# An output product with eleven matmuls for twelve, and a filter product with its constants as weights

## The chip, the cores and the metric

The kernel runs on one core of one Trainium2 chip. The metric is the device time of one execution in microseconds. Several executions are timed, and the median counts. One more execution is recorded by the profiler. The engines have short names in the profile: PE (the matrix engine, PEld its weight loads), DVE (vector), ACT (scalar, here the exponentials), POOL, and SP, which mainly starts transfers.

## The reference

Two independent branches have their results put side by side. Sizes: S = 2048 positions, D = 448 features, H = 16 heads of Dh = 28.

```
# A: attention with 16 query heads and one shared key and value head
q = (A_x @ A_wq) in 16 heads;  k = A_x @ A_wk;  v = A_x @ A_wv
p = softmax(q @ k.T * Dh**-0.5)          # per head, 2048 x 2048
a = concat over heads(p @ v) @ A_wo
# B: a filter in the frequency domain, over positions and features
b = irfft2(rfft2(B_x) * (B_w_r + 1j*B_w_i))
return concat([a, b], axis=-1)           # 1 x 2048 x 896, float32
```

## The kernel before

**Opening.** In the first 70 us an explicit planner (class `Plan`) orders the projections of queries, keys and values, and the first transforms of the filter. Products that must be exact to float32 are made of float32r parts: a number x becomes a high part (x cast to float32r) and a low part (x minus that), and three products stand for one: high by high, low by high, high by low. A float32r product is one matmul record in the profile. A plain float32 product is two records.

**Attention loop.** The 2048 queries are four chunks c of 512, the 16 heads four groups g of four heads. Each of the 16 pairs (c, g) has 16 steps, one for each 128 keys: 256 steps. A step has four scores (`score`, L1100: 128 keys by 512 queries, float32r), four exponentials on ACT (L1117, from a PSUM bank to a buffer p in SBUF, of which there are `P_BUFS`), and four value products (`values`, L1132, float32, each in its own 32 columns of the array, so that the four run side by side). The values of a group add up in bank 7. DVE copies it out (`group_out`), POOL carries the row sums through DRAM and back as a tile R, with transfers that spread each sum over 32 rows, and `group_norm` multiplies by 1/sum and splits the result into `oh` and `ol`. A head occupies 32 rows of these tiles: 28 of results, one with the sum, three spare.

**Filler.** Two more kinds of PE work are cut into pieces and put between scores by `fill`. An output unit (`w_unit`, 12 of them: three chunks of four blocks of 128 positions; L1020) has four pieces, one for each group, of three float32r matmuls of 448 columns (`oh` by `woh`, `ol` by `woh`, `oh` by `wol`, where `woh` and `wol` are the parts of the output weights). The last chunk's output products for groups 0 to 2 run at the very end. The last transforms of the filter have units in two stages, 16 of each: `z_unit` (L942) goes over positions, four float32 products of 128 columns; `y_unit` (L961) over features, four float32 products of 113 columns with the data as weights and the constants `cs3` streaming. DVE then combines the four results (L966 to L975), and SP stores them to `ob`. Before that, DVE has done a transform over the 32 residues and the filter's weights on a tile X, as background work up to about 310 us.

**Order.** The loop at the end of the kernel fixes the order of every engine when the program is built. It keeps clocks of its own for PE, DVE and ACT (`clk`), a time for each bank to come free (`free`), and a heap of later work (`after`). It writes the values of `n` steps at once, a *round*, where `size` makes n four if more than 1 us of filler is ready, else two. After each round `share` sets how much filler the next may take: at least 1.6 us, or the rest spread over the remaining steps. `LEAD` is how many scores run ahead of a round. Each engine then executes its list in order.

Of the kernel before, what the change touches and what calls it, by code (L numbers as in the profile page):

```python
# [12 lines left out]
F32 = mybir.dt.float32  # L13
F32R = mybir.dt.float32r
# [3 lines left out]
ALU = mybir.AluOpType  # L18
# [5 lines left out]
DH = D // H  # L24
# [7 lines left out]
P_BUFS = 20  # L32
# [63 lines left out]
def kernel(ctx: ExitStack, tc: tile.TileContext, t: dict):  # L96
# [14 lines left out]
    X = cp.tile([128, 2, 32, 113], F32, name="X")  # L111
# [101 lines left out]
    with tc.tile_pool(name="f1", bufs=2) as f1[0], tc.tile_pool(name="w1", bufs=1) as w1, ExitStack() as ctx1:  # L213
# [146 lines left out]
        def load_const(name, shape):  # L360
            def go():
                cons[name] = cp.tile(shape, F32, name=name)
                nc.sync.dma_start(cons[name], t[name])
            return add(SP, 0.4, go, loads[1, 1], kb=32)
# [297 lines left out]
    pp = ctx.enter_context(tc.tile_pool(name="pp", bufs=P_BUFS))  # L662
    V = nc.vector
# [27 lines left out]
    woh = ap.tile([128, NG, D], F32R, name="woh", bufs=1)  # L691
    wol = ap.tile([128, NG, D], F32R, name="wol", bufs=1)
    fc["cs3"] = ap.tile([113, 4, 113], F32, name="cs3", bufs=1)
    nc.gpsimd.dma_start(fc["cs3"], t["cs3"])
# [214 lines left out]
    Xf = X.rearrange("p r n f -> p (r n f)")  # L909
    taken = [0]  # L910

    def carve(p, n):
        o = taken[0]
        taken[0] += n
        return Xf[:p, o:o + n]

    c2t = [carve(128, 904).rearrange("p (u j f) -> p u j f", u=2, f=113) for _ in range(2)]
    fit = [carve(128, 512).rearrange("p (j f) -> p j f", f=128) for _ in range(2)]
    zt = [[carve(113, 512).rearrange("p (r j n) -> p r j n", r=2, n=64) for _ in range(2)] for _ in range(2)]
    mt = [carve(128, 226).rearrange("p (k f) -> p k f", f=113) for _ in range(2)]  # L920
    y1t = [carve(128, 452).rearrange("p (k h f) -> p k h f", k=2, f=113) for _ in range(2)]
    yot = [carve(128, 452).rearrange("p (k f) -> p k f", f=113) for _ in range(2)]
# [6 lines left out]
    def fft3_load(q):  # L929
        if q > 7:  # L930
            return
        nc.gpsimd.dma_start(c2t[q % 2].rearrange("p u j f -> p u (j f)"), t2[:, :, 452 * q:452 * q + 452])
        nc.gpsimd.dma_start(fit[q % 2], t["fi"][:, 4 * q:4 * q + 4])
        after(clk["dve"] + (10.0 if q < 2 else 6.0), 0.0, work["z"].extend, [z_unit(q, 0), z_unit(q, 1)])

    def z_unit(q, e):
        w = (113, 112)[e]

        def go(b):
            pz = view(bank[b], 4, 128)  # L940
            for j in range(4):
                mm(pz[:w, j], c2t[q % 2][:, e, j, :w], fit[q % 2][:, j], start=True, stop=True)  # L942
            if e == 1:
                after(clk["pe"] + 1.2, 0.0, fft3_load, q + 2)
            after(clk["pe"] + 1.2, 0.72, out, b)

        def out(b):
            V.tensor_copy(zt[q % 2][e][:w], view(bank[b], 4, 128)[:w].rearrange("p j (r n) -> p r j n", r=2))  # L948
# [3 lines left out]
        return [(0.88, go)]  # L952

    def y_unit(q, v):
        js = slice(2 * v, 2 * v + 2)

        def go(b):
            py = view(bank[b], 4, 113)
            ze, zo = zt[q % 2]
            for k, (z, w, r) in enumerate(((ze, 113, 0), (zo, 112, 0), (zo, 112, 1), (ze, 113, 1))):  # L960
                mm(py[:, k], z[:w, r, js], fc["cs3"][:w, k], start=True, stop=True)  # L961
            after(clk["pe"] + 1.2, 1.2, out, b)

        def out(b):
            py, m, y1 = view(bank[b], 4, 113), mt[v], y1t[v]
            V.tensor_copy(m, py[:, 2:4])  # L966
            TT(y1[:, :, 0], py[:, 0:2], m, op=ALU.add)
            TT(y1[:, :, 1], py[:, 0:2], m, op=ALU.subtract)
            free[b] = clk["dve"] + 0.1
            after(clk["dve"], 0.8, last)  # L970

        def last():
            y1, yo = y1t[v], yot[v]
            TT(yo[:, 0:2], y1[:, 0], y1[:, 1], op=ALU.add)
            TT(yo[:, 2:4], y1[:, 0], y1[:, 1], op=ALU.subtract)  # L975
            r0 = (2 * q + v) * 128
            nc.sync.dma_start(t["ob"][r0:r0 + 128], yo)
        return [(0.88, go)]


    oh, ol, osb = {}, {}, {}
# [13 lines left out]
    def group_sums(c, g, rs, rd):  # L995
        V.reciprocal(rs, rs)
        nc.gpsimd.dma_start(rd.rearrange("i (a b) -> (i a) b", b=16), rs)
        R = ap.tile([128, CW], F32, name="R", bufs=1)
        for i in range(4):
            nc.gpsimd.dma_start(R[32 * i:32 * i + 32], rd[i:i + 1].to_broadcast([32, CW]))  # L1000
        after(clk["dve"] + 12.0, 2.1, group_norm, c, g, R)

    def group_norm(c, g, R):
# [4 lines left out]
        TT(o, o, R, op=ALU.mult)  # L1008
        h = oh[c][:, g]
        V.tensor_copy(h, o)  # L1010
        TT(ol[c][:, g], o, h.bitcast(F32), op=ALU.subtract)
        normed[c] += 1
        if normed[c] == NG and c < NC - 1:
            after(clk["dve"] + 0.3, 0.0, work["w"].extend, [w_unit(c, k) for k in range(4)])

    def wo_mm(p, c, k, gs):
        s = slice(k * 128, k * 128 + 128)
        for g in gs:
            for n, (x, w) in enumerate(((oh, woh), (ol, woh), (oh, wol))):
                mm(p, x[c][:, g, s], w[:, g], start=(g == 0 and n == 0), stop=(g == NG - 1 and n == 2))  # L1020
# [20 lines left out]
    def w_unit(c, k):  # L1041
        def go(g):
            def f(b):
                wo_mm(bank[b][:, :D], c, k, (g,))
                if g == NG - 1:
                    after(clk["pe"] + 0.9, 0.65, out, b)
            return f

        def out(b):
            wo_out(bank[b][:, :D], c, k)  # L1050
            free[b] = clk["dve"] + 0.1
        return [(0.605, go(g)) for g in range(NG)]
# [102 lines left out]
    for g in range(NG):  # L1155
        after(w0 + 6 * g, 0.0, wo_load, g)
        after(w0 + 6.0 + 6 * g, 1.1, wo_split, g)
# [81 lines left out]
    nc.sync.dma_start(w3, t["wo"][:, g])  # L1239
# [69 lines left out]
def _layout(A_x, A_wq, A_wk, A_wv, A_wo, B_x, B_w_r, B_w_i):  # L1309
# [13 lines left out]
    z["wo"] = wo.reshape(NG, 128, D).transpose(1, 0, 2)  # L1323
# [18 lines left out]
def _gather(oa, ob):  # L1342
    out = np.empty((1, S, 2 * D), np.float32)
    out[0, :, :D] = oa
    y = ob.reshape(32, 64, 4, 113).transpose(1, 0, 2, 3).reshape(S, 4, 113)
# [9 lines left out]
_OUTS = {"oa": (S, D), "ob": (S, 4, 113)}  # L1355
# [16 lines left out]
```

## Time and profile before

| | |
|---|---|
| Median of three runs (lowest, highest) | 641.86 us (641.53, 643.83) |
| Profiled execution: time, span | 641.98 us, 640.1 us |
| Granted PE clock | 0.999 |
| Busy: PE, PEld | 633.5 us (99%), 358.5 us (56%) |
| Busy: ACT, DVE, POOL | 547.0 us (85%), 333.3 us (52%), 89.1 us (14%) |
| Transfers | 62.41 MB, mean 98 GB/s |

The span is the time from the first to the last instruction of the profiled execution, and the 1.9 us beside it lie around it. A line number names a line of the kernel before. In groups of the profile a tile is given by the name with which it was made, so the small tiles carved out of X are called X there.

### The profile page before, as it was taken

The page shows a single profiled execution, that of the slowest core. Times are in us where ns is not written, and L with a number is a line of the kernel's source. Part 1 is how long each engine was busy: PE and PEld are TensorE (multiplying, and loading weights), DVE is VectorE, ACT ScalarE, POOL GpSimd, SP SyncE. Part 2 cuts the span into 40 slices and gives each one's busy share as a digit, 9 for nine tenths or more (in the row PEclk, how much of TensorE's full clock was granted, in tenths as well). Part 3 has the DMA queues.
Part 4 walks back from the last instruction along what each step waited for, and adds up shares of the span by engine and source line. Part 5 has one row for each costly group of instructions (what it writes and reads, how often), then busy time and mean ns, then how long its engine had stood idle before and what let it go on. Part 6 is the DMA issues. An engine that isn't in the chain of part 4 may idle for free.

```text
span 640.1 us, 11636 instructions
## 1 busy us (share of the span) xinstructions
PE 633.5 (99%) x4380; PEld 358.5 (56%) x4380; DVE 333.3 (52%) x687; ACT 547.0 (85%) x1100; POOL 89.1 (14%) x164
## 2 busy tenths in 40 slices
PE   9999999999999999999999999999999999999997
PEld 7877544444444456554446655655665655564445
DVE  5999615979897977896323222215334310320014
ACT  4644899999999998889999879878888987888991
POOL 1021131101121101010122020020301101020200
PEclk9999999999999999999999999999999999999999
DMA  8766587030334121124444231132415131130002
GB/s 299 255 164 166 134 239 244 18 68 17 97 105 102 42 68 47 32 67 150 151 141 139 64 91 36 49 111 88 115 61 143 32 82 32 50 93 1 19 0 87
DMA packets 29667, 62.41 MB, mean 98 GB/s; under 512 B 6798, under 2 KB 18415, under 8 KB 28645
## 3 DMA queue, kind: packets, MB, share of 16 engines
q1 hardware_dynamic: 21850, 40.36, 23.1%
q0 software_dynamic: 7328, 20.72, 10.8%
q8 instruction: 35, 0.57, 0.4%
q10 hardware_dynamic: 432, 0.57, 0.3%
q14 instruction: 22, 0.18, 0.1%
HBM read 29.63 MB, written 15.02 MB: 70 GB/s over the span
## 4 chain that ended last, share of the span: by engine, by line
PE 88%; ACT 0%; issue 0%; DVE 0%; ACTq 0%
PE b L1100 41%; PE b L1132 36%; PE b L1020 6%; PE b L961 2%; PE b L942 2%; PE b L1252 0%; PE b L163 0%; ACT yb L1035 0%; DVE yb L1038 0%; ACTq L1036 0%
## 5 line engine op out<-in xcount | busy, mean ns | idle before, releaser
L1117 ACT ACTIVATE p<-b 128x512 f32<-128x512 f32 x1024 | 506.7, 768 | 46.4 <-PE b L1100 45.4
L1100 PE MATMUL b<-qa,ka 128*128 128x512 f32 x1024 | 284.7, 411 | 0.5 <-PEq L617 0.5
L1100 PEld LDWEIGHTS b<-qa,ka 128*128 128x128 f32 x1024 | 182.1, 188 | 128.2 <-ACT p L1117 83.9
L1132 PE MATMUL b<-p,vs 128*32 128x512 f32 x2048 | 240.0, 597 | 0.0
L1132 PEld LDWEIGHTS b<-p,vs 128*32 128x32 f32 x2048 | 56.5, 109 | 120.9 <-issue 119.3
L986 DVE COPY qraw<-b 128x512 f32<-128x512 f32 x15 | 10.4, 692 | 82.0 <-PE b L1132 82.0
L1024 DVE COPY ya<-b 128x448 f32<-128x448 f32 x12 | 7.5, 624 | 65.1 <-PE b L1020 64.0
L991 POOL DMA_DIRECT2D sd<-qraw x15 | 8.8, 587 | 218.8 <-DVE qraw L986 218.8
L827 DVE SCALAR_TENSOR_TENSOR X<-w,X 128x226 f32<-128x226 f32 (+2 forms) x72 | 34.1, 473 | 2.4
L1000 POOL DMA_DIRECT2D R<-rd x60 | 30.2, 508 | 34.9 <-DMA rd<-rs 34.9
L966 DVE COPY X<-b 128x226 f32<-128x226 f32 x16 | 6.2, 390 | 45.3 <-ACT p L1117 43.9
L321 ACT ACTIVATE qraw<-b 128x512 f32<-128x512 f32 x16 | 9.4, 599 | 19.5 <-PE b L317 19.4
L948 DVE COPY X<-b 113x512 f32<-113x512 f32 (+1 forms) x16 | 11.1, 691 | 28.6 <-ACT p L1117 22.7
L317 PE MATMUL b<-xh,wqh 128*128 128x512 f32 x64 | 24.6, 416 | 0.4 <-DVE xh L265 0.4
L1008 DVE TENSOR_TENSOR qraw<-qraw,R 128x512 f32<-128x512 f32 x15 | 10.3, 685 | 26.7 <-DMA R<-rd 26.7
L317 PE MATMUL b<-xh,wql 128*128 128x512 f32 x64 | 23.0, 390 | 0.0
L1020 PE MATMUL b<-woh,oh 128*128 128x448 f32 x60 | 22.1, 369 | 0.0
L1020 PE MATMUL b<-wol,oh 128*128 128x448 f32 x60 | 22.0, 366 | 0.0
L1020 PE MATMUL b<-woh,ol 128*128 128x448 f32 x60 | 21.9, 366 | 0.0
L820 DVE SCALAR_TENSOR_TENSOR w<-X 128x113 f32<-128x113 f32 (+2 forms) x56 | 17.7, 353 | 0.1
L961 PEld LDWEIGHTS b<-cs,X 113*128 113x128 f32 (+1 forms) x128 | 16.8, 191 | 1.4
L317 PE MATMUL b<-xl,wqh 128*128 128x512 f32 x48 | 17.3, 391 | 0.0
(113 smaller groups left out, 511.4 us busy)
## 6 DMA issues: line engine op xcount, KB each, us to landing
qa<-qa SPq DMA_DIRECT2D x15, 512.0 KB
X<-t POOLq DMA_DIRECT2D x16, 452.0 KB, 5.4
xb<-xb SPq DMA_DIRECT2D x8, 512.0 KB
qa<-qh SPq DMA_DIRECT2D x60, 64.0 KB
qa<-ql SPq DMA_DIRECT2D x60, 64.0 KB
R<-rd POOLq DMA_DIRECT2D x60, 64.0 KB, 2.2
t<-bs SPq DMA_DIRECT2D x16, 226.0 KB
wf<-w POOLq DMA_DIRECT2D x8, 452.0 KB, 4.2
```

What stands on the lines that cost most here:

```text
L317: mm(pq[c, g], w[:, j, gs], x[:, j], start=(j == 0 and n == 0), stop=(j == 3 and n == 1))
L820: STT(out, y, sy, x, op0=ALU.mult, op1=ALU.add if c > 0 else ALU.subtract)
L827: todo(226 * n, lambda d=d, q=q: STT(both(d), t[0].rearrange("p r n f -> p r (n f)"), q, both(a), op0=ALU.mult, op1=ALU.add))
L942: mm(pz[:w, j], c2t[q % 2][:, e, j, :w], fit[q % 2][:, j], start=True, stop=True)
L948: V.tensor_copy(zt[q % 2][e][:w], view(bank[b], 4, 128)[:w].rearrange("p j (r n) -> p r j n", r=2))
L961: mm(py[:, k], z[:w, r, js], fc["cs3"][:w, k], start=True, stop=True)
L986: V.tensor_copy(o, bank[7])
L1000: nc.gpsimd.dma_start(R[32 * i:32 * i + 32], rd[i:i + 1].to_broadcast([32, CW]))
L1020: mm(p, x[c][:, g, s], w[:, g], start=(g == 0 and n == 0), stop=(g == NG - 1 and n == 2))
L1100: mm(bank[b], ka[:, kc * 128:(kc + 1) * 128], qa[c, g][:, h], start=True, stop=True)
L1117: nc.scalar.activation(p, bank[b], AF.Exp, scale=SCALE)
L1132: mm(bank[7][32 * i:32 * i + 32], vs[:, kc], pt.pop(4 * st + i), start=(kc == 0), stop=(kc == 15))
```

## The change

**Eleven for twelve.** For the first three chunks the product of `ol`, group 0, by `woh` is no longer a matmul of its own. Its 16 heads' worth of rows (four heads of 28 rows, 112) are moved into the spare rows of seven other tiles: four rows of each head's 32 in `oh` for four groups and in `ol` for groups 1 to 3. To that end `ol` of group 0 is stored to DRAM (`lows`) by SP, and when group 3 is done eight small copies bring it back, after which the units become ready 7.0 us later by the planner's clock instead of 0.3. R now has 28 rows a head, with zeros in the rest from one memset. The weights get three further tiles (`woh` has 7 entries) whose spare rows hold the weights of group 0; they are loaded and split between 84 and 102 us on the planner's clock.

**Constants as weights.** `y_unit` now has the constants, split into `csh` and `csl`, as weights, and the data of `z_unit`, split into `zh` and `zl` by DVE, streaming: two sums of three float32r products, 256 columns each. The results are combined in two steps into whole blocks of 113 by 512 (`yo`) and stored as such; the host's gathering is fitted to it.

**Room.** X no longer has a place for the whole program: it lies in a pool of its own, which is closed when the last transforms begin, and their tiles take that place. `P_BUFS` goes from 20 to 17. The planner's numbers are fitted (a unit's pieces 0.403 and 0.605, 0.73 for the second filter product, at least 1.8 us of filler a round).

```diff
-P_BUFS = 20
+P_BUFS = 17
...
     def wo_split(g):
         V.tensor_copy(woh[:, g], wo[g])
-        TT(wol[:, g], wo[g], woh[:, g].bitcast(F32), op=ALU.subtract)
+        if g < NG:
+            TT(wol[:, g], wo[g], woh[:, g].bitcast(F32), op=ALU.subtract)
...
+    def fft3_open():
+        xp.close()
+        p3 = xp.enter_context(tc.tile_pool(name="p3", bufs=2))
...
+        cs = scratch()[:113, :452].rearrange("p (k f) -> p k f", k=4)
+        nc.gpsimd.dma_start(cs, t["cs3"])
+        todo(452, lambda: V.tensor_copy(csh, cs))
+        todo(452, lambda: TT(csl, cs, csh.bitcast(F32), op=ALU.subtract))
...
         def out(b):
-            V.tensor_copy(zt[q % 2][e][:w], view(bank[b], 4, 128)[:w].rearrange("p j (r n) -> p r j n", r=2))
+            pz = view(bank[b], 4, 128)[:w].rearrange("p j (r n) -> p r j n", r=2)
+            h, l = (x[:w] for x in fb["z", q % 2, e])
+            V.tensor_copy(h, pz)
+            TT(l, pz, h.bitcast(F32), op=ALU.subtract)
...
         def go(b):
-            py = view(bank[b], 4, 113)
-            ze, zo = zt[q % 2]
-            for k, (z, w, r) in enumerate(((ze, 113, 0), (zo, 112, 0), (zo, 112, 1), (ze, 113, 1))):
-                mm(py[:, k], z[:w, r, js], fc["cs3"][:w, k], start=True, stop=True)
-            after(clk["pe"] + 1.2, 1.2, out, b)
+            py = view(bank[b], 2, 256)
+            for k in range(2):
+                kind, e, r = ((0, 0, 0), (2, 1, 1), (1, 1, 0), (3, 0, 1))[2 * v + k]
+                w = (113, 112)[e]
+                zh, zl = (x[:w, r].rearrange("p j n -> p (j n)") for x in fb["z", q % 2, e])
+                for n, (c, z) in enumerate(((csh, zh), (csh, zl), (csl, zh))):
+                    mm(py[:113, k], c[:w, kind], z, start=(n == 0), stop=(n == 2))
+            after(clk["pe"] + 1.2, 2.65 if v else 1.25, out, b)
...
-        if normed[c] == NG and c < NC - 1:
-            after(clk["dve"] + 0.3, 0.0, work["w"].extend, [w_unit(c, k) for k in range(4)])
+        if c < NC - 1:
+            if g == 0:
+                lows[c] = dp.tile([128, CW], F32, name="lows", bufs=2)
+                nc.sync.dma_start(lows[c], ol[c][:, 0].bitcast(F32))
+            rows = lows[c].rearrange("(i m r) n -> r i m n", i=4, r=4)
+            if g == NG - 1:
+                for r in range(4):
+                    nc.sync.dma_start(oh[c][DH + r::32].bitcast(F32), rows[r, :, :4])
+                    nc.sync.dma_start(ol[c][DH + r::32, 1:].bitcast(F32), rows[r, :, 4:7])
+                after(clk["dve"] + 7.0, 0.0, work["w"].extend, [w_unit(c, k) for k in range(4)])
 
     def wo_mm(p, c, k, gs):
         s = slice(k * 128, k * 128 + 128)
         for g in gs:
-            for n, (x, w) in enumerate(((oh, woh), (ol, woh), (oh, wol))):
-                mm(p, x[c][:, g, s], w[:, g], start=(g == 0 and n == 0), stop=(g == NG - 1 and n == 2))
+            spare = c < NC - 1
+            for n, (x, w, m) in enumerate(((oh, woh, g), (oh, wol, g), (ol, woh, g + 3 * spare))):
+                if n < 2 or g or not spare:
+                    mm(p, x[c][:, g, s], w[:, m], start=(g == 0 and n == 0), stop=(g == NG - 1 and n == 2))
...
-    total = 12 * 4 * 0.605 + 32 * 0.88
+    total = 12 * 2.22 + 16 * (0.88 + 0.73)
 
     def share(n):
-        return max(1.6, n * (total - done[0]) / max(250 - done_steps, 3)) if n > 2 else 0.0
+        return max(1.8, n * (total - done[0]) / max(250 - done_steps, 3)) if n > 2 else 0.0
```

**The order.** Up to the 80th step PE and ACT have the same lists in both kernels. From there they part. On PE, the first output unit of the kernel before, between scores (L1100) of the round behind step 80:

```order
L1020 MATMUL b_80<-woh,oh 128x448
L1020 MATMUL b_80<-woh,ol 128x448
L1020 MATMUL b_80<-wol,oh 128x448
L1100 MATMUL b_81<-qa_1163,ka 128x512
L1100 MATMUL b_82<-qa_1163,ka 128x512
L1020 MATMUL b_80<-woh,oh 128x448
L1020 MATMUL b_80<-woh,ol 128x448
L1020 MATMUL b_80<-wol,oh 128x448
```

The same unit in the changed kernel (L1044; L1124 are the scores), which stands two rounds of two steps later, behind step 84:

```order
L1044 MATMUL b_78<-woh,oh 128x448
L1044 MATMUL b_78<-wol,oh 128x448
L1124 MATMUL b_80<-qa_1167,ka 128x512
L1124 MATMUL b_81<-qa_1167,ka 128x512
L1044 MATMUL b_78<-woh,oh 128x448
L1044 MATMUL b_78<-wol,oh 128x448
L1044 MATMUL b_78<-woh,ol 128x448
```

The first piece has two products, each later one three. Next on PE, the round of four steps that ends at step 204 in the kernel before, with two units of the second filter product in it (cs and X are the constants and the data carved from X; x4 are four products). The value products close the round: x16 for four steps, x8 for two.

```order
L1100 MATMUL b_79<-qa_128,ka 128x512
L961 MATMUL b_81<-cs_1092,X 128x113 x4
L1100 MATMUL b_82<-qa_128,ka 128x512
L1100 MATMUL b_77<-qa_128,ka 128x512
L961 MATMUL b_83<-cs_1092,X 128x113 x4
...
L1100 MATMUL b_78<-qa_128,ka 128x512
L1132 MATMUL b_84<-p,vs 32x512 x16
```

The place ahead of step 204 in the changed kernel, a round of two steps without filler:

```order
L1156 MATMUL b_83<-p,vs 32x512 x8
L1124 MATMUL b_79<-qa_127,ka 128x512
L1124 MATMUL b_82<-qa_127,ka 128x512
...
L1124 MATMUL b_79<-qa_127,ka 128x512
L1156 MATMUL b_83<-p,vs 32x512 x8
```

And its first unit of the second filter product, behind step 134:

```order
L972 MATMUL b_77<-zh_3809,csh 113x256
L972 MATMUL b_77<-zl_3810,csh 113x256
L972 MATMUL b_77<-zh_3809,csl 113x256
L972 MATMUL b_77<-zh_3811,csh 113x256
L972 MATMUL b_77<-zl_3812,csh 113x256
L972 MATMUL b_77<-zh_3811,csl 113x256
```

Four products of 113 columns have become six of 256. Counted over PE's list the loop has 30 rounds of four steps and 68 of two before, 23 and 82 now. Before, the steps from 128 to 204 are nineteen rounds of four; now those from 188 to 212 are twelve rounds of two with no filler between. At the end, six output products stand in the last round before and 33 behind the last values, now three and 36. On SP, ahead of the query copies for the next group (L206), the changed list has the copies into the spare rows:

```order
L207 DMA qa_1167<-qa_1167 64x2048
L1034 DMA oh<-lows 4x4x512
L1035 DMA ol<-lows 4x3x512
L1034 DMA oh<-lows 4x4x512
L1035 DMA ol<-lows 4x3x512
...
L206 DMA qa_127<-qh 32x512
L206 DMA qa_127<-ql 32x512
```

Four pairs of them stand there for each of the first three chunks.

More of the change, by code (lines that the diff above doesn't have):

```diff
@@ new lines, in go @@
+            after(clk["pe"] + 1.2, 2.65 if v else 1.25, out, b)
+        def out(b):
+            py = view(bank[b], 2, 256)[:113]
+            y = y1[v] = scratch()[:113, :768].rearrange("p (s n) -> p s n", s=3)
+            V.tensor_copy(y[:, 2], py[:, 1])
+            TT(y[:, 0], py[:, 0], y[:, 2], op=ALU.add)
+            TT(y[:, 1], py[:, 0], y[:, 2], op=ALU.subtract)
+            free[b] = clk["dve"] + (-1.3 if v else 0.1)
+            if v:
+                a, c = y1.pop(0), y1.pop(1)
+                for h, op in enumerate((ALU.add, ALU.subtract)):
+                    last(h, op, a, c)
@@ L982, with last @@
+        def last(h, op, a, c):
+            yo = fp.tile([113, 2, 256], F32, name="yo", tag="bs")
+            TT(yo, a[:, :2], c[:, :2], op=op)
+            nc.sync.dma_start(t["ob"][q, h], yo)
+        return [(0.73, go)]
+    oh, ol, osb, lows = {}, {}, {}, {}
+    R = ap.tile([128, CW], F32, name="R", bufs=1)
+    after(12.0, 0.4, V.memset, R, 0.0)
     normed, taken_out = [0] * NC, [0]
@@ L1051, in out @@
             free[b] = clk["dve"] + 0.1
-        return [(0.605, go(g)) for g in range(NG)]
+        return [(0.605 if g else 0.403, go(g)) for g in range(NG)]
     def switch(mode):
@@ L1154 @@
     w0 = 5.0 if FIRST == 8 else 28.0
-    for g in range(NG):
-        after(w0 + 6 * g, 0.0, wo_load, g)
-        after(w0 + 6.0 + 6 * g, 1.1, wo_split, g)
+    for g in range(7):
+        at = w0 + 6 * g if g < NG else 60.0 + 6 * g
+        after(at, 0.0, wo_load, g)
+        after(at + 6.0, 1.1, wo_split, g)
     for q in range(FIRST, 8):
```

72 lines of the change are left out of this document (28 added, 44 removed).

## The prediction

> **What bounds the kernel now.** I read the page first: its busy times and the chain that ended last.
>
> ```profile
> span 640.1 us, 11636 instructions
> PE 633.5 (99%) x4380; PEld 358.5 (56%) x4380; DVE 333.3 (52%) x687; ACT 547.0 (85%) x1100; POOL 89.1 (14%) x164
> PE 88%; ACT 0%; issue 0%; DVE 0%; ACTq 0%
> ```
>
> The matrix engine is occupied for 99% of the span, and the chain runs through it almost without a break. A busy PE may still be a waiting one, so I went on to the chain in order of time, where each piece ends when the next begins. One round of the attention loop from 397.43, and ahead of it a filter piece of the round before, with the scores behind it:
>
> ```profile
> 392.99 0.88 PE b L961 x8
> 393.87 0.48 PE b L1100 x2
> ...
> 397.43 3.57 PE b L1132 x32
> 401.00 1.59 PE b L1100 x6
> 402.59 0.60 PE b L1020 x3
> 403.19 0.45 PE b L1100 x2
> 403.65 0.62 PE b L1020 x3
> 404.27 0.46 PE b L1100 x2
> 404.73 0.87 PE b L942 x8
> 405.60 1.42 PE b L1100 x6
> 407.02 3.57 PE b L1132 x32
> ```
>
> L1132 are the value products of four steps (a full-fp32 product shows as two records, so x32 is 16 products), L1100 the scores, L1020 the output product, L942 and L961 the filter's first and second product of its last transform. Everything stands back to back: the round lasts 407.02 - 397.43 = 9.59 us, and its pieces add up to that. So each microsecond of filler taken from PE is worth up to a microsecond here. Without its filler this round is 3.57 + 1.59 + 0.45 + 0.46 + 1.42 = 7.49 us. A score costs 0.46 / 2 = 0.23, an output product about 0.61 / 3 = 0.205, and a second filter product (four fp32 products) 0.88, plus 0.02 that the two scores behind it take longer (0.48 against 0.46): 0.90.
>
> Not all rounds are of four steps. The planner makes rounds of two steps where no filler is ready; here is one before the first output products and one after them:
>
> ```profile
> 227.27 2.04 PE b L1100 x8
> 229.31 1.85 PE b L1132 x16
> ...
> 278.86 2.11 PE b L1100 x8
> 280.96 1.85 PE b L1132 x16
> ```
>
> Two such rounds do the attention work of one four-step round, and take 2 x (2.11 + 1.85) = 7.92 us late, 2 x (2.04 + 1.85) = 7.78 early, against 7.49. The turns between scores and values are paid twice. This is the row on which the argument hangs, since the change alters the number of rounds.
>
> Where does PE wait? In the rounds that hold the first output products the last run of scores is stretched:
>
> ```profile
> 235.51 1.63 PE b L1100 x5
> ...
> 245.05 1.69 PE b L1100 x6
> ...
> 254.66 1.68 PE b L1100 x6
> ...
> 264.27 1.91 PE b L1100 x7
> ...
> 274.11 1.18 PE b L1100 x5
> ```
>
> Five scores take 1.18 at 274.11 and 1.63 at 235.51; six take 1.42 at 405.60 and 1.69 and 1.68 here; seven should take 1.65 and take 1.91. That is 0.45 + 0.27 + 0.26 + 0.26 = 1.24 us in which a score waits for a bank that an exponential has not read yet. ACT is the second limit, and close.
>
> **The change part by part.** *Output product.* The order of PE has eleven products in each of the twelve units (three chunks of four) instead of twelve; all have 448 columns as before. Twelve products of 0.205 go: -2.46 us.
>
> *Second filter product.* A unit was four fp32 products (0.90 us); it becomes six fp32r products of 256 columns. No row has an fp32r product of 256 columns. The nearest are the 0.205 of 448 and the 0.23 of 512 columns. In proportion they give 0.117 and 0.115, a straight line through both 0.13; I take 0.12, which makes 0.72 a unit. As bounds serve 0.87 / 8 = 0.109, which each of the eight fp32 records at 404.73 took with a weight load of its own, and 0.205, if nothing is saved by the fewer columns. The 16 units save 16 x (0.90 - 0.72) = 2.88 us; with the bounds 16 x 0.25 = 4.0 saved, or 16 x 0.33 = 5.3 lost. The Trainium skill, page "TensorE: Matmul & The Clock Gate", Part 1, has back-to-back products at N / 2.4 GHz plus about 2.5 ns, and measures 215.7 ns at 512 columns. The rows above give 230 for those, so the trace does not agree, being 14 ns a product slower. By that rule a 256-column product would take 109 ns, an estimate from the page, and the sum below would come out 1.1 us lower.
>
> *Rounds.* In the order of PE the loop has 30 four-step and 68 two-step rounds before, 23 and 82 now: there is less filler, it is spread at 1.8 us a round at least instead of 1.6, and the outputs of a chunk become ready later, so it runs out sooner. Seven four-step rounds turn into fourteen. One of these pairs stands ahead of the first output (0.29), six behind it (7.92 - 7.49 = 0.43): 0.29 + 6 x 0.43 = +2.87 us. This eats more than half of what the products give. With the early price for all seven it is 2.0.
>
> *Waits.* The four rounds with the first outputs now carry 11 output products instead of 9, that is 0.41 us more PE work each, where a round waited 0.26 to 0.45. I let the 1.24 us go: -1.24, with 0 as the one bound. The other bound is -2.2, since the long rounds later (17 scores with two L942 pieces) may hold a further microsecond of small gaps that I cannot lay on single rows.
>
> *Fewer probability buffers, 17 for 20.* ACT in the rounds around 397:
>
> ```profile
> 391.87 6.47 ACT L1117 ACTIVATE p<-b 128x512 f32<-128x512 f32 x13 [1.16 <-PE b L1100]
> 398.50 1.57 ACT L1117 ACTIVATE p<-b 128x512 f32<-128x512 f32 x3 [0.16 <-PE b L1132]
> 401.47 6.47 ACT L1117 ACTIVATE p<-b 128x512 f32<-128x512 f32 x13 [1.39 <-PE b L1100]
> ```
>
> At 398.50 ACT waited for the values (L1132) to give a buffer back, then did three, and from about 400.1 it idled 1.39 us for new scores. With three buffers fewer it stops three exponentials earlier, and these come after the release instead: 3 x 0.48 = 1.44 us of work into a hole of 1.39. Cost nothing, as long as that hole covers it; a two-step round asks for 8 + 7 = 15 buffers at most, under 17. This cover is thin, and is a rival below.
>
> *Spare rows through DRAM.* Per chunk one store and eight small copies on SP's queue, 27 in all, and the units wait for them. The rows for their price are the last operand of group (1,0) on DVE, the first output product, and on SP's queue the last of eight copies with the copy that waits for it:
>
> ```profile
> 222.56 0.69 DVE L1011 TENSOR_TENSOR ol<-qraw,oh 128x512 fp32r<-128x512 f32 x1
> ...
> 232.74 0.61 PE b L1020 x3
> ...
> 332.62 0.59 SPq L207 DMA_DIRECT2D qa<-ql  x1
> 335.60 0.50 SPq L208 DMA_DIRECT2D qa<-qa  x1
> ```
>
> Eight issues of 0.59 are 4.7 us, and landing takes 335.60 - 333.21 = 2.4: the rows are there at about 223.25 + 7.1 = 230.4. The order puts the first output two two-step rounds later than before, near 232.7 + 7.8 = 240.5. Ten microseconds of cover: cost nothing. Queued behind the eight copies are the query copies of the next group, which come 4.7 us later; the kernel builds them a whole group ahead.
>
> *DVE.* Its nearest rows, with a stretch of the filter's last transform:
>
> ```profile
> L948 DVE COPY X<-b 113x512 f32<-113x512 f32 (+1 forms) x16 | 11.1, 691 | 28.6 <-ACT p L1117 22.7 <-PE b L942 5.9
> 400.00:450.00 50.00, 50.00 (x333) 30.25 (x326) 14.60 (x29) 41.05 (x84) 6.70 (x12) 1.00 0.29 83
> 322.85 0.69 DVE L1008 TENSOR_TENSOR qraw<-qraw,R 128x512 f32<-128x512 f32 x1 [12.86 <-DMA R<-rd]
> ```
>
> The first product's result is now cast and subtracted, so up to 0.69 more for each of 16 units, 11 us on an engine (the third figure with a count in the stretch's row) that was busy for 14.60 us of those 50. The constants' load and split fall where DVE stood 12.86 us for another transfer. Cost nothing; without such cover 0.69 a unit, 11 us. POOL's new loads stand among transfers that PE does not wait for.
>
> *End.* The last round loses three output products and the tail behind the last values gains three, 0.62 each way: nothing, or +0.6 if the last exponentials hold the round anyway.
>
> The sum: -2.46 - 2.88 + 2.87 - 1.24 = -3.71 us. The profiled execution took 641.98 us, its span 640.1 and 1.9 around it, and is 0.12 above the median of the three runs, 641.86. So 638.3 us, 0.56% under the median. A measurement of this kernel can tell about 0.5% (3.2 us) from no change, so the forecast lies just beyond what can be told.
>
> **The rivals.** *First, the second filter product saves nothing.* If the weight loads are not hidden behind so short a stream and a product takes 0.15, six take 0.90, and the sum is -0.83: 641.2 us, no change. For it speaks that a load lasts longer than the stream of 256 columns:
>
> ```profile
> L942 PEld LDWEIGHTS b<-X x128: 173/177/178, 336.6 to 534.3; 128*113 128x113 f32 x64, 128*112 128x112 f32 x64
> ```
>
> Against it, eight of just these loads with their products passed in 0.87 us, so 0.177 of span overlaps to 0.109. The Trainium skill, page "TensorE: Matmul & The Clock Gate", section "Weight-path perf modes", turns its fast weight load on only for weights of 128 columns that are not FP32. By that rule the new weights, 113 wide, load slowly, like the L942 ones, whose loads the trace shows overlapped.
>
> *Second, slower: the load is laid bare.* At 0.205 a product a unit takes 1.23, the 16 lose 5.28 where I have 2.88 gained, and the sum is +4.45: 646.4. It decides from 0.159 a product (sum zero); 3.2 us slower needs 0.192. The same overlap speaks against it.
>
> *Third, slower: too few buffers.* If the release comes later than the hole allows, every four-step round is longer by it. At 0.30 us late the 23 rounds lose 6.9, and the time is 645.2. The hole is 1.39 for 1.44, so it starts at once, but PE's own work in these rounds has grown and hides some.
>
> *Fourth, slower: PE waits for the spare rows.* Beyond ten microseconds of delay in each of three places each further one costs one; 3.2 slower needs 2.3 past the cover three times.
>
> **How the numbers follow.** Forecast 0.62; no saving in the filter 0.20; bare loads 0.06; buffers 0.06; spare rows 0.03; something else that ends near no change 0.03. The forecast's own spread (waits stay, end +0.6) leaves 0.08 of its 0.62 above 638.65, within 0.5%. Faster by more: 0.54. Same: 0.08 + 0.20 + 0.03 = 0.31. Slower: 0.15. The range starts at 635.4: waits at -2.2 (1.0 lower), rounds at the early price (0.9 lower), products at 0.109 (1.0 lower). It ends at 641.5, just above the first rival, and leaves out the three slower cases and little below.
>
> **What would show it.** In the changed trace six fp32r products of the filter should take 0.72 us in the chain, an output unit 11 x 0.205, a four-step round without filler 7.49, a late two-step round 3.96, and the stretched scores behind the first outputs should be gone. ACT's hole ahead of new scores should shrink to nearly nothing and not turn into waits of scores for exponentials. Wrong I am if a filter product takes 0.15 or more, if the two-step rounds shrink below 3.9, or if PE stands ahead of an output unit.

## Result, and the profile after

The changed kernel takes 681.91 us (median of six runs, 678.92 to 682.71), against 641.86 us of the kernel before: a ratio of 1.0615, interval 1.0589 to 1.0640. The forecast was 638.3 us in a range of 635.4 to 641.5. The profiled span of the changed kernel is 678.8 us.

Its page, first the engines' busy times and then the chain that ended last:

```profile
span 678.8 us, 11646 instructions
PE 635.8 (94%) x4336; PEld 355.3 (52%) x4336; DVE 347.5 (51%) x693; ACT 547.8 (81%) x1100; POOL 90.4 (13%) x167
PE 70%; DMA 16%; DVE 2%; issue 1%; ACT 0%; POOL 0%; ACTq 0%; DVEq 0%; POOLq 0%
PE b L1124 34%; PE b L1156 30%; DMA ob<-yo 16%; PE b L1044 5%; PE b L946 1%; PE b L972 1%; DVE yo L989 0%; PE b L1277 0%; DMA rs<-sd 0%; DVE zh L954 0%; DVE zl L955 0%; PE b L162 0%; ACT yb L1059 0%; DVE w L978 0%; DVE w L979 0%
```

Before, PE held 88% of the chain and no transfer appeared in it. Now PE stands idle for 43 us (678.8 - 635.8) where it was 6.6 before, and 16% of the chain is one kind of transfer: `ob<-yo`, the stores of the filter's results. How they stop PE is read backwards. First PE in time, from the end of one round to the first scores of the next (start, length, instructions, and in brackets the idle time ahead with its releaser):

```profile
481.80 3.64 PE L1156 MATMUL b<-p,vs 128*32 128x512 f32 x32
502.29 1.22 PE L1124 MATMUL b<-qa,ka 128*128 128x512 f32 x2 [16.85 <-DVE zl L955]
```

PE waits 16.85 us until DVE has split a first filter product (L954 to L955), because the next score goes into that product's bank. DVE in the same stretch:

```profile
490.59 0.69 DVE L989 TENSOR_TENSOR yo<-w 113x512 f32<-113x512 f32 x1 [11.21 <-DMA ob<-yo]
500.21 0.69 DVE L989 TENSOR_TENSOR yo<-w 113x512 f32<-113x512 f32 x1 [8.94 <-DMA ob<-yo]
500.82 0.68 DVE L954 CAST zh<-b 113x512 fp32r<-113x512 f32 x1
501.54 0.69 DVE L955 TENSOR_TENSOR zl<-b,zh 113x512 fp32r<-113x512 f32 x1
```

DVE executes its list in order, and the split stands behind the additions that fill `yo` (L989). Of `yo` there are two buffers, and each addition waits until an earlier block's store has read its buffer. Summed over the run, in the waits of DVE and of PE (total, times, longest):

```profile
DVE yo L989 <- DMA ob<-yo: 48.9, 7, 11.2
PE b L1124 <- DVE zl L955: 32.3, 3, 16.8
```

And in the chain in order of time the stores stand one behind the other:

```profile
426.67 24.98 DMA ob<-yo
...
452.39 21.41 DMA ob<-yo
...
476.95 23.24 DMA ob<-yo
...
500.93 17.35 DMA ob<-yo
```

Each of these pieces is a pair of stores in flight. In the records of single packets a store is 113 packets of 2048 bytes, one for each row; between 479.6 and 519.9 us there are 477 of them at a mean of 86.7 ns, that is 41.3 us of packets in 40.3 us of time. So they went through one at a time, about 10 us a store, at 2048 bytes in 86.7 ns, 24 GB/s. The packets of a store of the kernel before, 128 rows of 1808 bytes, passed side by side: where a store stood alone, all 128 were through within 0.75 us, with 13 in flight in the mean. Five rounds of the loop are stretched by it (16.8, 11.9, 30.0, 13.1 and 11.1 us long), and the loop from its third round to its last values lasts 582.3 us, against 537.4 with the stores mended (below). That is 44.9 us, and the device times of the two differ by 44.6 (681.91 - 637.35).

Not all of it is standstill. Between the pages of the changed kernel and of the mended one, PE is idle 36.7 us longer (43.0 against 6.3) and busy 6.8 us longer (635.8 against 629.0) for the same 4336 matmuls. In three stretches of the changed kernel PE's granted clock is half (the last figure but two of each row; the first after the comma is PE's busy time):

```profile
368.59:382.25 13.66, 5.56 (x19) 2.75 (x23) 3.56 (x6) 3.53 (x7) 0.00 (x0) 0.50 0.10 33
488.06:508.54 20.48, 6.15 (x19) 4.81 (x20) 5.15 (x9) 4.24 (x8) 0.00 (x0) 0.50 0.09 31
518.78:525.61 6.83, 3.45 (x15) 1.39 (x19) 4.80 (x9) 1.58 (x3) 0.00 (x0) 0.50 0.07 28
```

Each begins 1.9 to 2.6 us after PE has come to stand for 5 us or more, and ends 3.4 to 6.3 us after it runs again. The two scores of 1.22 us above show it, where two take 0.62 in a row of this kind at 348.79, and so does the round of 13.1 us from 502.29, in which PE doesn't stand at all: the mended kernel's takes 10.1. PE was busy for 15.2 us of these stretches; at full clock that would be 7.6, an estimate, and so the clock can account for the 6.8.

### The profile page after: what moved, and what is told of

It is laid out like the page before. It is cut to its first block, busy times and chain, and to the rows that moved or that the text cites. A ratio compares the mean times of both kernels' runs of the same rounds, so it can differ in the third digit from the quotient of the medians.

```text
span 678.8 us, 11646 instructions
## 1 busy us (share of the span) xinstructions
PE 635.8 (94%) x4336; PEld 355.3 (52%) x4336; DVE 347.5 (51%) x693; ACT 547.8 (81%) x1100; POOL 90.4 (13%) x167
## 4 chain that ended last, share of the span: by engine, by line
PE 70%; DMA 16%; DVE 2%; issue 1%; ACT 0%; POOL 0%; ACTq 0%; DVEq 0%; POOLq 0%
PE b L1124 34%; PE b L1156 30%; DMA ob<-yo 16%; PE b L1044 5%; PE b L946 1%; PE b L972 1%; DVE yo L989 0%; PE b L1277 0%; DMA rs<-sd 0%; DVE zh L954 0%; DVE zl L955 0%; PE b L162 0%; ACT yb L1059 0%; DVE w L978 0%; DVE w L979 0%
## 5 line engine op out<-in xcount | busy, mean ns | idle before, releaser
L1124 PE MATMUL b<-qa,ka 128*128 128x512 f32 x1024 | 287.6, 413 | 35.9 <-DVE zl L955 32.3
L1124 PEld LDWEIGHTS b<-qa,ka 128*128 128x128 f32 x1024 | 183.9, 190 | 165.7 <-ACT p L1141 85.2
L1156 PE MATMUL b<-p,vs 128*32 128x512 f32 x2048 | 243.5, 602 | 0.0
L989 DVE TENSOR_TENSOR yo<-w 113x512 f32<-113x512 f32 x16 | 10.8, 691 | 49.1 <-DMA ob<-yo 48.9
L978 DVE COPY w<-b 113x256 f32<-113x256 f32 x16 | 6.8, 424 | 35.8 <-PE b L972 32.1
L1044 PE MATMUL b<-woh,oh 128*128 128x448 f32 x60 | 22.0, 367 | 0.0
L1044 PE MATMUL b<-wol,oh 128*128 128x448 f32 x60 | 22.0, 367 | 0.0
L946 PE MATMUL b<-fi,c 128*112 128x128 f32 (+1 forms) x128 | 16.7, 273 | 1.3 <-DVE zl L955 1.3
L946 PEld LDWEIGHTS b<-fi,c 128*112 128x112 f32 (+1 forms) x128 | 16.0, 177 | 3.2 <-DVE zl L955 1.7
L1044 PE MATMUL b<-woh,ol 128*128 128x448 f32 x48 | 17.6, 366 | 0.0
```

What stands on the lines that cost most here:

```text
L946: mm(pz[:w, j], fb["c2", q % 2][:, e, j, :w], fb["fi", q % 2][:, j], start=True, stop=True)
L989: TT(yo, a[:, :2], c[:, :2], op=op)
L1044: mm(p, x[c][:, g, s], w[:, m], start=(g == 0 and n == 0), stop=(g == NG - 1 and n == 2))
L1124: mm(bank[b], ka[:, kc * 128:(kc + 1) * 128], qa[c, g][:, h], start=True, stop=True)
L1156: mm(bank[7][32 * i:32 * i + 32], vs[:, kc], pt.pop(4 * st + i), start=(kc == 0), stop=(kc == 15))
```

## Experiments

The kernels ran in three sets (1 to 4, 5 to 8, 9 to 12), and each ratio is against runs of the kernel before on the same chip in the same set (medians 642.25, 643.65 and 643.26 us).

**1. The same rows in two stores.**

```diff
-            nc.sync.dma_start(t["ob"][q, h], yo)
+            nc.sync.dma_start(t["ob"][q, h, :112], yo[:112])
+            nc.sync.dma_start(t["ob"][q, h, 112:], yo[112:])
```

> The changed kernel, but each store of a 113-row block to ob is two: 112 rows and 1 row, with the same rows of 2048 bytes at the same places. Theory A (the store of 113 rows runs its packets one after another on a single DMA engine, because 113 is prime; the vector engine then stands for the store's buffer, and the matrix engine behind it): the landing falls from 10 us and more to about 2, the waits of DVE for ob (48.9 us) and of PE for DVE vanish, and the five stretched rounds come back to their sums, 44.8 us less: about 636 us. Rival B (the layout of ob or the 2 KB rows make the store slow): nothing changes, 678 us or more. Rival C (stores stand in SP's queue behind the copies into the spare rows): not better, with 16 more issues on the queue, 680 us.

Measured: 637.35 us (635.97 to 637.70), ratio 0.9916 (0.9899 to 0.9932). Span and chain on its page:

```profile
span 635.3 us, 11665 instructions
PE 88%; ACT 0%; issue 0%; DVE 0%; ACTq 0%
```

One store more each, and 44.6 us are gone; no wait of DVE for `ob` is left. It is neither the layout of the block nor the place in SP's list, but the count of 113 rows.

**2. The store of 113 rows, unsplit, from POOL's queue** (`nc.gpsimd.dma_start` in place of `nc.sync.dma_start`).

> The changed kernel with the 16 stores of 113 rows issued by POOL instead of SP, unsplit. Theory A (a single engine for a 113-row transfer of SP's queue): in the changed trace POOL's transfer of 113 rows for the constants ran on all engines in 5 us, so the stores land in 3 to 6 us and most of the stall goes: 635 to 645 us. Rival B (layout of ob): still 20 us for a pair of stores and about 680 us. Rival C (SP's order): stall gone as well, but each store lands no faster than the 10 us of the changed kernel.

Measured: 637.01 us (one run). The tile's view, time from issue to landing:

```profile
DMA to landing us min/median/max: 2.6/3.4/5.6
```

The same 113 rows land in 3.4 us when POOL issues them, so the slowness belongs to this count on SP's queue.

**3. 106 and 7 rows from SP** (106 and 7 in place of 112 and 1).

> As the 112-row split, but 106 rows and 7 rows. 106 is 2 x 53. Theory A in its full form (as many engines as the largest number up to 16 that divides the rows): 106 packets of 2 KB over two engines at 92 ns each, about 4.9 us a store, 10 for a pair; PE stalls only where units stand close, 636 to 645 us. If A is only about an odd number of rows, 106 rows go over all engines in under 1 us and the time is that of the 112-row split, about 636. Rivals B and C: 678 or more.

Measured: 644.91 us (one run). On its page the transfer is back in the chain, at a quarter of its share:

```profile
PE 82%; DMA 4%; DVE 1%; SPq 1%; issue 0%; ACT 0%; ACTq 0%; DVEq 0%
```

112 rows are fast, 106 in between, 113 slow. The Trainium skill, page "DMA: Bandwidth & Descriptors", section "Why a DMA increments its semaphore by 16 and not by 1", says that a transfer goes to k DMA engines, k being the largest number up to 16 that divides the slowest dimension (other than 1) on both of its sides, so that 127 partitions go to one engine, and that some direct copies issued by POOL are excepted and get 16. All three runs agree: 112 is divisible by 16, 106 by 2, 113 by nothing, and POOL's store of 113 took 3.4 us. That it is two engines for 106 rows is inferred, since the records don't name the engine; but the packets in flight can be counted. Where a pair of stores stood alone, it was 2.0 to 2.3 in the mean here, 9 to 11 in number 1, and 1.0 over the stretch of the changed kernel above. POOL's stores differ in one more thing: their packets have 4096 bytes.

**4. The kernel before with its 128 rows stored as 127 and 1.**

```diff
-            nc.sync.dma_start(t["ob"][r0:r0 + 128], yo)
+            nc.sync.dma_start(t["ob"][r0:r0 + 127], yo[:127])
+            nc.sync.dma_start(t["ob"][r0 + 127:r0 + 128], yo[127:])
```

> The kernel before, with each store of 128 rows to ob split into 127 rows and 1 row. 127 is prime. Theory A: 127 packets of 1808 bytes at 76 ns, 9.7 us a store on one engine and 19.4 for a pair, where pairs come every 18.7 us in the dense part: landing grows from about 2 to 10 and 20 us, DVE waits a few us for buffers, and little reaches PE: 642 to 650 us. Rival B: packets spread over all engines as before, no wait of DVE for ob, 642 us. Rival C: 16 more issues on SP, no more: 642 us.

Measured: 660.27 us (one run), 18 us more than the kernel before: the sign is as expected, the size above the range. (Its granted clock is 0.989: here too PE's clock halves around standstills.) In its view of the tile `ob`, the issues on SP's queue (ns, min/median/max), and in DVE's waits:

```profile
L978 SPq DMA_DIRECT2D ob<-X x16: 542/7880/10914, 350.3 to 590.8; - x16
DVE X L974 <- DMA ob<-X: 39.6, 6, 7.9
```

What I had left out: the second, one-row store holds SP itself for a median of 7.88 us, and the query copies queued behind it come late too (`qa<-ql` stands in this kernel's chain). So a slow row count costs twice, through the buffer and through the queue. But it needs nothing else of the change: the kernel before falls into it as well.

With the store mended, the rest of the change can be judged against the forecast. 637.35 us lies within 1 us of the forecast sum, so I next tried its terms one at a time, expecting them to add up. They did not.

**5. The mended kernel with the old least filler** (`max(1.6, ...)` in place of 1.8 in `share`).

> The changed kernel with 112 + 1 rows a store, and the least filler of a four-step round at 1.6 us again instead of 1.8. The order of PE then has 28 four-step and 72 two-step rounds instead of 23 and 82: five pairs of two-step rounds fewer, the same products. If the number of rounds costs what the profile before says (0.29 to 0.43 us a pair), 1.5 to 2.1 us less than the 637.35 of the 112-row split: 635.2 to 635.9. Rival (ACT limits rounds with little filler, so that the turns saved come back as waits for banks): no change, 637.0 to 637.7.

**6. Eleven products for twelve alone**: the filter as before, 17 buffers, 1.6 us of filler.

```diff
-            for n, (x, w) in enumerate(((oh, woh), (ol, woh), (oh, wol))):
-                mm(p, x[c][:, g, s], w[:, g], start=(g == 0 and n == 0), stop=(g == NG - 1 and n == 2))
+            spare = c < NC - 1
+            for n, (x, w, m) in enumerate(((oh, woh, g), (oh, wol, g), (ol, woh, g + 3 * spare))):
+                if n < 2 or g or not spare:
+                    mm(p, x[c][:, g, s], w[:, m], start=(g == 0 and n == 0), stop=(g == NG - 1 and n == 2))
```

> The kernel before with only the eleven output products for twelve (spare rows, R with 28 rows a head, seven weight tiles, 17 buffers); the filter's last product and its stores as before, least filler 1.6. PE's order has 30 four-step and 68 two-step rounds as before. By the sum: 12 x 0.205 = 2.46 us less, up to 3.7 if the waits behind the first outputs go too: 638.5 to 639.8 against 642.25 before. Rival (the spare rows through DRAM are waited for): no gain, 642 or more, and PE idle ahead of an output unit.

**7. The filter product alone** (constants as weights, stores of 112 and 1 rows, twelve output products, 17 buffers, 1.6 us).

```diff
-                mm(py[:, k], z[:w, r, js], fc["cs3"][:w, k], start=True, stop=True)
+                for n, (c, z) in enumerate(((csh, zh), (csh, zl), (csl, zh))):
+                    mm(py[:113, k], c[:w, kind], z, start=(n == 0), stop=(n == 2))
```

> The kernel before with only the filter's last product turned round (constants as weights, six fp32r products of 256 columns, 112 + 1 rows a store, 17 buffers); output product of twelve, least filler 1.6. PE's order has 28 four-step and 72 two-step rounds. By the sum: 16 x 0.19 = 3.0 us less (a product measured 0.118), and two pairs of rounds more, 0.6 to 0.9: 639.8 to 640.2 against 642.25 before. Rival (more DVE work a unit delays PE): 642 or more.

**8. The kernel before with 17 buffers** (`P_BUFS = 17`).

> The kernel before with 17 probability buffers instead of 20, nothing else; the order of PE has the same 30 and 68 rounds. If the hole of ACT ahead of new scores takes the three moved exponentials: no change, 641.9 to 642.6. Rival (too few buffers): up to 0.3 us for each of 30 four-step rounds, 643 to 651.

Measured for 5 to 8:

| | us | ratio |
|---|---|---|
| 5, mended, 1.6 us | 641.93 | 0.9975 (0.9956 to 0.9994) |
| 6, outputs alone | 643.13 | 0.9989 (0.9967 to 1.0010) |
| 7, filter alone | 642.21 | 0.9973 (0.9955 to 0.9991) |
| 8, before, 17 buffers | 642.88 | 0.9976 (0.9954 to 0.9999) |

The buffers cost nothing, as forecast: number 8 has the loop of the kernel before (543.6 us, table below). As its ratio is 0.9976 all the same, ratios this near to one can't be told from none, and the loops of the profiled executions have to decide. Number 7 is within its interval of the 2.1 to 2.4 us that were expected. But number 6 gains nothing where 2.5 to 3.7 us were expected, and number 5, which was to be a little better than the mended kernel, is worse: with 5.5 us of PE's work saved it gains 1.6 us. So PE's work alone isn't what sets these rounds, and I asked again what does. The answer was in the trace of before, in a view that I had not cut by the kind of round: the busy times of one stretch of two-step rounds alone, and of one of (nearly only) four-step rounds (length, then busy time and count of PE, PEld, DVE, ACT, POOL; PE's clock):

```profile
133.10:223.28 90.18, 90.18 (x557) 42.39 (x553) 77.42 (x158) 90.18 (x187) 14.68 (x27) 1.00 0.31 76
372.15:513.66 141.51, 141.51 (x947) 85.49 (x944) 47.26 (x107) 119.49 (x240) 19.81 (x36) 1.00 0.29 81
```

PE is "busy" for every microsecond of both. ACT is busy for all 90.18 of the first and for 119.49 of 141.51 (84%) of the second. In a two-step round ACT is the bound: eight exponentials in 3.92 us, 0.49 each. In a four-step round it stands still for a while, because the values take PE for 3.57 us and no new scores come. A matmul that waits for its bank counts as busy, and so PE's 99% said nothing. A record of ACT might be stretched likewise, so its spacing is the better sign: over the trace of before half of the exponentials begin 0.477 to 0.479 us after the one ahead, and eight of these are 3.8 of the 3.92 us. No run shortened the exponentials: that it is ACT that sets the floor is argued from this, not tested.

Theory P from this: a four-step round lasts at least its 16 exponentials and the gap, about 9.6 us, whatever filler is in it up to some 2.1 us (9.6 - 7.49); only what goes beyond that is paid. Two tests on it, and the best form once more:

**9. The kernel before with 2.2 us of least filler** (`max(2.2, ...)` in place of 1.6): no product saved, but 23 four-step rounds instead of 30.

> The kernel before with at least 2.2 us of filler a round instead of 1.6, and nothing else: no product is saved, but its loop has 23 rounds of four steps and 82 of two, as the changed kernel has. Theory P (a four-step round lasts as long as the longer of two things: its 16 exponentials and the gap behind them, about 9.60 us, or its work on PE, 7.49 us and the filler; a saved product counts only in a round above that floor): the 23 rounds have 57.2 / 23 = 2.49 us of filler and come to 9.98, the 82 take 3.964, together 554.6 where the kernel before has 30 x 9.469 + 68 x 3.979 = 554.6. So no change, -1 to +1.5 us. Theory Q (denser packing by itself is the gain): 3 to 4 us faster. Theory R (the prediction's separate terms, the turns paid +2.9 and no wait gone): +2.9.

Measured: 641.50 us, ratio 0.9966 (0.9952 to 0.9981), 2.2 us less; its profiled loop is 0.9 us shorter. That is between P and Q by the times and P by the trace, and against R: fewer four-step rounds are no loss.

**10 and 11. Number 5 and number 1 with four of the six products of each second filter unit left out**:

```diff
-                for n, (c, z) in enumerate(((csh, zh), (csh, zl), (csl, zh))):
-                    mm(py[:113, k], c[:w, kind], z, start=(n == 0), stop=(n == 2))
+                for n, (c, z) in enumerate(((csh, zh),)):
+                    mm(py[:113, k], c[:w, kind], z, start=(n == 0), stop=(n == 0))
```

> As e7_share16, but every second filter product keeps only its high by high part: four of six products of a unit are left out, 64 x 0.118 = 7.55 us of work of PE, and the order is otherwise the same. Theory P: nearly all rounds of this order stand on the floor of 9.59 (16 exponentials) or 9.11 (15) in the trace of e7_share16; only the five with two units of it and one of the first product stand above, by 0.2 to 0.35. So about 1.0 to 1.5 us less than e7_share16 had against the kernel before: 640.4 to 641 where that had 641.9, and rounds of 9.6 that stay at 9.6. Theory R (PE's work sets every round): 7.5 us less, 634.4.

> As e1_rows112, but every second filter product keeps only its high by high part: four of six products of a unit are left out, 64 x 0.118 = 7.55 us of work of PE, and the order is otherwise the same. Theory P: the rounds with such units stand at 9.60 to 10.14 in the trace of e1_rows112, a little above the floor of 9.60 (16 exponentials) or 9.11 (15): they fall to it, 0.06 to 0.55 each, 2.0 us in all. So 635.4 where e1_rows112 had 637.35. Theory R: 7.5 less, 629.8.

**12. The changed kernel with the stores issued by POOL**, in rounds.

> The changed kernel with its 16 stores of 113 rows issued by POOL instead of SP, as in e2_pool_store, now timed in rounds beside the others: it is the plainest of the mended forms and stands for e1_rows112 on this chip. All theories: as e1_rows112, a ratio of 0.992 (0.990 to 0.993), 4.5 to 6 us faster than the kernel before.

Measured:

| | us | ratio |
|---|---|---|
| 10, number 5, products left out | 639.91 | 0.9940 (0.9921 to 0.9959) |
| 11, number 1, products left out | 636.89 | 0.9898 (0.9873 to 0.9923) |
| 12, stores from POOL | 636.90 | 0.9898 (0.9877 to 0.9920) |

Number 12 gains a little more than the 4.5 to 6 us expected. With 7.55 us of PE's work less, number 11 takes what number 12 takes. P had expected 2.0 us of gain there, R 7.5; none shows in the medians, and 0.3 us in the profiled loops. Number 10 gains 1.6 us on number 5 by the medians (each against its own set), where P had 1.0 to 1.5, while their profiled loops are 541.9 and 541.6 us: the traces show no gain. So R is refuted twice, and P is right in kind but not in size. The same round of 12 and of 11 in the chain in order of time shows where the products go; first 12:

```profile
428.25 1.59 PE b L1124 x6
429.84 0.72 PE b L972 x6
430.56 0.46 PE b L1124 x2
431.02 0.71 PE b L972 x6
431.74 0.47 PE b L1124 x2
432.20 0.87 PE b L946 x8
433.08 1.25 PE b L1124 x5
434.33 3.57 PE b L1156 x32
```

and 11 (all lines one further down in its code):

```profile
428.37 1.59 PE b L1125 x6
429.96 0.24 PE b L972 x2
430.21 0.47 PE b L1125 x2
430.67 0.35 PE b L972 x2
431.02 0.98 PE b L1125 x2
432.00 1.12 PE b L946 x8
433.12 1.33 PE b L1125 x5
434.45 3.57 PE b L1157 x32
```

From the first score to the values it is 6.08 us in both. The eight products left out here are worth 0.84 us; it comes back as two scores of 0.98 instead of 0.47, 1.12 for 0.87 and 1.33 for 1.25: matmuls that wait, for ACT by the theory, and are recorded as busy. The next round but one is plainer still: its filler is three second filter products in 12 (from 448.17; 3 x 0.71 = 2.13 us) and a third of each in 11 (from 448.29; 0.71 us of work), and it lasts 9.65 us in both.

The rounds of all the kernels, each from its first score to the next round's, from the third round on (two-step rounds without the first two), and the loop from there to the last values:

| | four-step: count, mean us | two-step: count, mean us | loop us |
|---|---|---|---|
| before | 30, 9.47 | 66, 3.93 | 543.6 |
| 8, before, 17 buffers | 30, 9.47 | 66, 3.93 | 543.6 |
| 6, outputs alone | 30, 9.48 | 66, 3.93 | 543.9 |
| 7, filter alone | 28, 9.55 | 70, 3.92 | 542.0 |
| 5, mended, 1.6 us | 28, 9.54 | 70, 3.92 | 541.6 |
| 10, as 5, products left out | 28, 9.53 | 70, 3.93 | 541.9 |
| 9, before, 2.2 us | 23, 10.00 | 80, 3.91 | 542.7 |
| 1, mended | 23, 9.78 | 80, 3.91 | 537.4 |
| 12, stores from POOL | 23, 9.78 | 80, 3.91 | 537.4 |
| 11, as 1, products left out | 23, 9.77 | 80, 3.90 | 537.1 |

Rows 8 and 6 have the same rounds, and fewer products change nothing. Rows 9 and 1 have the same numbers of rounds too (not the same filler in each), and there the products count nearly in full: 23 x (10.00 - 9.78) = 5.1 us of the 5.5 saved. In 9 the filler, 57.2 / 23 = 2.49 us a round by the planner's sum, stands above what the gap hides; in 6 and 8, with 1.9, below it. Row 11, with 1.92, is below it in the mean again, but its rounds stay at 9.77 and don't come down to 9.60. All that was left out lay in ten of its 23 rounds, and these became 0.4 us shorter together: they stood on a floor already, some above 9.60 (one of 9.80 with 16 exponentials). So there is a floor, but not one number for every order, and what sets it in these rounds stays open.

## Why the prediction was wrong

**The stores were never costed: this failed.** The prediction counts the added casts, constants, spare rows and waits, but of the stores to `ob` it says nothing, though the diff turns blocks of 128 rows into blocks of 113. It held that the extra work of DVE "cost nothing". DVE's work did cost nothing; its wait for the two `yo` buffers, in a list where the split that frees a bank of PE stands behind, cost 44.6 us (681.91 - 637.35): in the spans, 36.7 us of standstill of PE and 6.8 us of longer matmuls, with PE's clock halved around each long standstill. None of the four rivals was this one.

**The products.** Sizes right, use wrong. A second filter product shows six in 0.71 to 0.72 us, 0.118 to 0.12 each as taken (429.84 above) and not the 0.15 of the first rival, and an output unit two and then three at a time. But "each microsecond of filler taken from PE is worth up to a microsecond" was read from pieces that stand back to back, and does not hold: number 6 lost 12 products and gained 0.7 us, within its interval of none, with a loop of 543.9 us against 543.6, and number 11 gained nothing from 64 more.

**Rounds, +2.87.** Wrong sign. Set against the values, two two-step rounds are the dearer ones, 7.92 against 7.49; but no four-step round lasted 7.49. It lasts about 9.6 with 2.1 us of filler as with 0.7 (no run had one without), and two two-step rounds last about 7.82. So it costs some 1.7 us more than two two-step rounds instead of 0.43 less, and carries 2 us of filler for that. Going from 30 to 23 gave 0.9 us in the loop by itself (number 9, where the filler then overflows the gap) and 6.2 us together with the products.

**Waits, -1.24.** They went, as forecast, and gave nothing. In number 12 the last four scores of the rounds with the first outputs take 0.92 to 0.93 us, 4 x 0.23, in three of four (1.15 in the first). But these three rounds last 9.67 to 9.72 us, where those before with 16 exponentials lasted 9.60. So the waits are not a term beside the others. By theory P they are ACT's floor, seen where a round has little filler; that is inferred.

**Buffers, spare rows, DVE, end.** These held: 17 buffers have 0.9976 (0.9954 to 0.9999) and the same rounds, neither PE nor an output unit waits for the spare rows, and in number 1 PE never stands for the split. From the last values to the end of the span it is 14.1 us before and 14.4 in number 1.

So the mended kernel's gain on the first chip (0.9916, 5.4 us) stands near the forecast's 3.7 for a reason that the forecast did not have: it counted the saved products as a gain by themselves and fewer four-step rounds as a loss, and by the runs these two errors pull opposite ways. The nearness is luck. That three of its terms lean on each other was visible only when they were run apart.

## What to carry to other kernels

When a change alters the shape of a store, cost it like an instruction: its row count, the queue that issues it, how many buffers stand behind it, and what follows in the list of the engine that waits for these buffers. When an engine is busy 99% of the time, cut its stretches by kind and see whether another is busy at 100% in one of them; then take work out of the first, and look at whether the time follows. Savings under such a floor are worth only what is packed above it, so the packing is tuned together with them: the best form here is the change with the stores issued by POOL (or split as 112 and 1 rows), 0.9898 (0.9877 to 0.9920) of the time before.

## What the runs showed of the hardware

A store of 226 KB took about 10 us as 113 rows from SP's queue, and 3.4 us as the same 113 rows from POOL's. Stores of 113 and of 127 rows from SP sent their packets one at a time (86.7 ns for 2048 bytes at 113 rows); 106 rows lay in between, at 2.0 to 2.3 in flight; 112 and 128 did not stall anything. A one-row store issued behind a slow one held SP for 7.88 us (median). PE's granted clock was half in 41.0 us of the changed kernel, each stretch beginning 1.9 to 2.6 us after PE had come to stand. Matmuls that waited were recorded as longer matmuls (two scores 0.98 instead of 0.47 us), so that PE showed no idle time at all in a stretch where ACT was busy throughout (90.18 of 90.18 us). What stays open: two-step rounds settle at 3.89 to 3.93 us in some stretches and at 3.95 to 3.97 in others, in the kernel before and in the mended one, and no run told why; nor was it tested whether shorter exponentials would lower the floor of the four-step rounds.
